# Working out a token's norm, exponentials and gate where its expert works on it, and not where its attention row is finished

## The chip, the cores and the metric

The kernel runs on one core of one Trainium2 chip, as one launch. The metric is the device time of that launch in microseconds (us), lower is better. A run's time is that of the whole program; the span is the time from the first to the last instruction in the profile of one execution.

## The reference

Attention without a softmax feeds a mixture of eight experts, of which each token uses one. B = 8 batches, S = 2496 tokens, D = 256, d_qk = 64, E = 8 experts, F = 1024.

```
attn = maximum(z @ z.T / S, 0) ** 2          # per batch, 2496 x 2496, symmetric
x    = u * (attn @ v)                        # 19968 tokens x 256
xn   = x / (norm(x) + 1e-6);  en = expert_emb / (norm(expert_emb) + 1e-6)
logits = xn @ en.T / tau
e    = argmax(logits)
gate = exp(logits[e] - max) / (sum(exp(logits - max)) + 1e-9)
out  = gate * (maximum(x @ w1[e], 0) @ w2[e])
```

## The kernel before

There are two parts, one after the other. In both, values are split into a high and a low float16 half, so that a product takes three matmuls.

The attention part walks over 800 steps (b, g, s): 8 batches, 5 groups of query tokens (four of 512, one of 448), 20 blocks of 128 keys. In a step TensorE does the six matmuls of `values` into the two accumulators `acc` of the group, and, where the block isn't the transpose of one done before (`own`), the two of `scores` for a block five ahead. ScalarE takes the ReLU and the square (L303, L307), VectorE makes the halves (L314, L315). The order of the instructions on ScalarE, VectorE and SyncE is the order of the program (`manual_schedule`); nothing overtakes on these three.

When a group's last step is done, `route` gives a list of pieces, each with a number of steps after which it is put into the program: x = u * acc (`gate_x`), sum of squares for a common power of two (`squares`, `total`, `scale`), the halves (`high`, `low`), four DMA transposes into whole rows (`turn`), the logits (`logits`, `take`), the argmax (`top`), the place in the expert's list (`rank`, `place`), and then the row's norm (`sums`, `norm`, `root`, `roots`), its exponentials (`shifted`, `exps`) and its gate (`gates`). At last `scatters` writes each token's row, 256 words of x in halves and 4 of tail, to its place in the DRAM tensor `xs` by an indirect DMA of GpSimd. The pieces of one group lie over the steps of the next two and more. One PSUM bank, `psM`, serves `rank`, the scales of z and v of the next batch, and the scales of the expert weights; `pm_free` keeps these apart.

The expert part takes slots of one expert's tokens: 61 of 256 tokens (A) and then 37 of 128 (B; four more are skipped here). `slot_x` loads a slot's tokens from `xs`, transposed, and their tails (`me`); `slot_w` loads 1 MB of weights, or leaves them if the expert is the same; `slot_up` does x @ w1 into `ph` tiles of 512 columns, ScalarE the ReLU (`hh`, L919) and VectorE the low half (`hl`, L920); `slot_down` does h @ w2, VectorE multiplies by the gate from `me` (`ot`, L945), and an indirect DMA writes the rows of `out`. `slot_down(k - 1)` follows `slot_up(k)`. After each `ph` tile and each half of `slot_down`, `pop` puts the next pieces of the last groups' `route` into the program. The buffers of the expert part lie where those of attention lay.

Of the kernel before, what the change touches and what calls it, by code (L numbers as in the profile page):

```python
# [19 lines left out]
P = 128  # L20
TA, TB = 256, 128
ROW = 260
# [23 lines left out]
def relu2_attention_then_moe(ctx, tc, zT, uT, v, emb, tau, w1, w2, ident, tri, iota_e, out):  # L46
# [309 lines left out]
    def route(b, g, acc, ut):  # L356
# [5 lines left out]
        xhl = rt.tile([P, 4, 512], F16, name="xhl", tag="xhl", bufs=1)  # L362
# [3 lines left out]
        n2 = rt.tile([P, 4], F32, name="n2", tag="n2")  # L366
        row = rt.tile([P, 4, ROW + 4], F32, name="row", tag="row", bufs=3)
        rowi = row.bitcast(I32)
# [34 lines left out]
        def logits():  # L403
            pm = acc[1]
            for j in range(nj):
                for q in range(4):
                    nc.tensor.matmul(pm[:, j * 2 * E:(j + 1) * 2 * E], xhl[:, q, j * P:(j + 1) * P], enhl[:, q % 2, :],
                                     start=(q == 0), stop=(q == 3))

        def rest_scale():  # L410
# [3 lines left out]
            odn = rt.tile([P, 1], F32, name="odn", tag="odn")  # L414
            nc.vector.tensor_tensor(odn, dn, oinv, op=ALU.mult)
            epu = rt.tile([P, 1], F32, name="epu", tag="epu")
            nc.vector.tensor_tensor(epu, up, eps, op=ALU.mult)
            loc.update(odn=odn, epu=epu)

        def take():  # L420
            pv = acc[1][:, 0:nj * 2 * E].rearrange("p (j c) -> p j c", c=2 * E)
# [4 lines left out]
            sh = rt.tile([P, 4, E], F32, name="sh", tag="sh")  # L426
            nc.vector.tensor_tensor(sh[:, :nj, :], lg[:, :nj, :], m[:, :nj].unsqueeze(2).broadcast_to([P, nj, E]), op=ALU.subtract)
            loc["sh"] = sh

        def top():  # L430
            sh = loc["sh"]
            cand = rt.tile([P, 4, E], F32, name="cand", tag="cand")
            nc.vector.scalar_tensor_tensor(cand[:, :nj, :], sh[:, :nj, :], 0.0, iotd[:, :nj, :], op0=ALU.is_ge, op1=ALU.mult)
# [11 lines left out]
        def sums():  # L445
            x = rt.tile([P, 4, D], F32, name="x", tag="xt", bufs=1)
            nc.vector.tensor_tensor(x[:, :nj, :], row16[:, :nj, 0:D], row16[:, :nj, D:2 * D], op=ALU.add)
            loc["x"] = x

        def norm(j):  # L450
            def f():
                sq = rt.tile([P, D], BF16, name="sq", tag="sq", bufs=1)
                nc.scalar.activation(sq, loc["x"][:, j, :], AF.Square, accum_out=n2[:, j:j + 1])
            return f

        def root():
            loc["root"] = sqrt_of(n2[:, :nj], (P, nj), "x")

        def roots():
            loc["s"] = loc["root"]()  # L460

        def shifted():
            inv = rt.tile([P, 4], F32, name="inv", tag="inv")
            nc.vector.tensor_scalar(inv[:, :nj], loc["s"], loc["epu"], None, op0=ALU.add)
            nc.vector.reciprocal(inv[:, :nj], inv[:, :nj])
            sh = loc["sh"]
            nc.vector.tensor_tensor(sh[:, :nj, :], sh[:, :nj, :], inv[:, :nj].unsqueeze(2).broadcast_to([P, nj, E]), op=ALU.mult)

        def exps():
            ex = rt.tile([P, 4, E], F32, name="ex", tag="ex")  # L470
            nc.scalar.activation(ex[:, :nj, :], loc["sh"][:, :nj, :], AF.Exp, scale=itau)
            loc["ex"] = ex

        def gates():
            sm = rt.tile([P, 4], F32, name="sm", tag="sm")
            nc.vector.tensor_reduce(sm[:, :nj], loc["ex"][:, :nj, :], axis=AX.X, op=ALU.add)
            nc.vector.tensor_scalar_add(sm[:, :nj], sm[:, :nj], 1e-9)
            nc.vector.reciprocal(sm[:, :nj], sm[:, :nj])
            nc.vector.tensor_scalar(row[:, :nj, D:D + 1], sm[:, :nj].unsqueeze(2), loc["odn"], None, op0=ALU.mult)
            nc.vector.tensor_scalar_add(rowi[:, :nj, D + 1:D + 2], idb[:, :nj].unsqueeze(2), float(b * S + t0))  # L480
            nc.gpsimd.memset(row[:, :, D + 2:ROW], 0.0)

# [9 lines left out]
        def place():  # L492
            ob, pm = loc["ob"], loc.pop("pm")
            state["pm"] = False
            old = state["carry"]
            pos = rt.tile([P, 4, E], F32, name="pos", tag="pos")
            nc.vector.tensor_tensor(pos[:, :nj, :], pm[:, 0:nj * E].rearrange("p (j e) -> p j e", e=E),
                                    old.unsqueeze(1).broadcast_to([P, nj, E]), op=ALU.add)
            new = sml.tile([P, E], F32, name="carry", bufs=3)
            nc.vector.tensor_tensor(new, pm[:, 4 * E:5 * E], old, op=ALU.add)  # L500
            state["carry"] = new
            nc.vector.tensor_tensor(pos[:, :nj, :], pos[:, :nj, :], ob[:, 4:4 + nj, :], op=ALU.mult)  # L502
            dst = rt.tile([P, 4], F32, name="dst", tag="dst")
            nc.vector.tensor_reduce(dst[:, :nj], pos[:, :nj, :], axis=AX.X, op=ALU.add)
            dsti = rt.tile([P, 4], U32, name="dsti", tag="dsti", bufs=3)
# [281 lines left out]
    tables = {}  # L787
    tiles = cst.tile([1, 1], I32, name="tiles")
# [57 lines left out]
    nc.vector.memset(pad.bitcast(I32)[:, D + 1:D + 2], N)  # L846
# [18 lines left out]
    def pop():  # L865
        state["step"] += 1
        run(state["step"])

# [3 lines left out]
    def slot_x(k):  # L872
# [3 lines left out]
        if k < XFIRST:  # L876
            xt = mx.tile([P, 4, T], F16, name="xt16", tag="xt16")
            me = mx.tile([P, T // P, ROW - D], F32, name="me", tag="me")
        else:
            xt = mst["mr"].tile([P, 4, T], F16, name="xr16", tag="xr16")  # L880
            me = mst["mr"].tile([P, T // P, ROW - D], F32, name="mer", tag="mer")
        nc.sync.dma_start_transpose(xt, xs[bass.ds(off, T), :].bitcast(F16)[:, 0:2 * D])
        nc.sync.dma_start(me, xs[bass.ds(off, T), D:ROW].rearrange("(j p) w -> p j w", p=P))
        mst["x", k] = xt, me
# [15 lines left out]
    def slot_up(k):  # L900
        mp, T = mst["mp"], slot_of(k)[2]
        wb = mst["w"][0][k % NWB]
        xt = mst["x", k][0]
# [21 lines left out]
    def slot_down(k):  # L925
# [3 lines left out]
        me = mst.pop(("x", k))[1]  # L929
# [3 lines left out]
        for j in range(nj):  # L933
# [8 lines left out]
            pop()  # L942
        for j in range(nj):
            o = po[:, j * D:(j + 1) * D]
            nc.vector.tensor_scalar(ot[:, j, :], o, me[:, j, 0:1], ws_, op0=ALU.mult, op1=ALU.mult)  # L945
            nc.gpsimd.indirect_dma_start(  # L946
                out, bass.IndirectOffsetOnAxis(ap=me.bitcast(U32)[:, j, 1:2], axis=0),
# [142 lines left out]
    def work(k0, k1, load=True):  # L1090
# [15 lines left out]
    ks = KT - NSKIP if KB > 2 * NSKIP else KT  # L1106
# [77 lines left out]
```

## Time and profile before

| | |
|---|---|
| runs | 2192.25, 2198.60, 2198.92 us; median 2198.6 us |
| profiled execution, its own time | 2194.44 us |
| its span | 2192.3 us |
| TensorE busy | 2100.9 us (96%) |
| VectorE busy | 1420.4 us (65%) |
| ScalarE busy | 1196.4 us (55%) |
| GpSimd busy | 352.5 us (16%) |
| mean granted TensorE clock | 0.991 of 2.4 GHz |

The profile is one execution. Busy shares over the whole span mix the two parts, so they have to be taken from stretches of time: attention runs from the start to 1334.8 us, the experts from there to the end. A busy TensorE may still be slowed by its clock, which is given beside it.

### The profile page before, as it was taken

What the parts mean: (1) busy time and instruction counts of PE and PEld (TensorE: products, weight loads), DVE (VectorE), ACT (ScalarE), POOL (GpSimd) and SP (SyncE); (2) the same over time, 40 slices, a digit from 0 to 9 for tenths busy, and PEclk for the clock granted to TensorE, in tenths of its full rate; (3) what the DMA queues carried; (4) which work ended last, traced back from release to release, by engine and by line L of the source; (5) the groups of instructions that cost most, each with busy time, mean ns of one, the idle gap of its engine ahead of it and who ended that gap; (6) DMA issues with size and microseconds to landing.
All of it is one profiled execution on the core that took longest, in us unless ns stands there. A gap on an engine that the chain in (4) does not pass through costs nothing. (4 is left out here: it accounts for less than half of the span.)

```text
span 2192.3 us, 43207 instructions
## 1 busy us (share of the span) xinstructions
PE 2100.9 (96%) x15154; PEld 1345.3 (61%) x15154; DVE 1420.4 (65%) x3796; ACT 1196.4 (55%) x2329; POOL 352.5 (16%) x428
## 2 busy tenths in 40 slices
PE   6999999999999999999999999999999999999997
PEld 2444444444444444444444446888888888889996
DVE  7788878888889878798888864543333333333332
ACT  6778768768868858768869762222222222221221
POOL 0011111111111111111111111221111111111111
PEclk9999999999999999999999999999999999999999
DMA  6766957975975965966976647443233332237360
GB/s 165 176 145 191 197 140 187 189 207 129 222 196 129 244 158 128 239 170 181 202 185 148 145 104 208 112 118 72 50 91 94 88 88 52 52 112 203 92 164 27
DMA packets 610316, 317.85 MB, mean 145 GB/s; under 512 B 530981, under 2 KB 573486, under 8 KB 602928
## 3 DMA queue, kind: packets, MB, share of 16 engines
q1 hardware_dynamic: 594912, 273.82, 53.5%
q0 software_dynamic: 15184, 41.24, 6.0%
q8 instruction: 121, 1.98, 0.4%
q14 instruction: 99, 0.81, 0.1%
HBM read 297.95 MB, written 59.60 MB: 163 GB/s over the span
## 5 line engine op out<-in xcount | busy, mean ns | idle before, releaser
L303 ACT ACTIVATE a<-sc 128x512 f32<-128x512 f32 (+1 forms) x480 | 277.7, 579 | 86.0 <-PE sc L301 81.7
L307 ACT ACTIVATE a<-a 128x512 f32<-128x512 f32 (+1 forms) x480 | 300.6, 626 | 15.1
L344 PEld LDWEIGHTS <-vv 128*128 128x128 f16 x1520 | 149.1, 98 | 193.3 <-issue 18.1
L512 POOL DMA_INDIRECT xs<-row,dsti x160 | 179.2, 1120 | 517.2 <-DMA xs<-row,dsti 314.5
L346 PEld LDWEIGHTS <-vv 128*128 128x128 f16 x1520 | 149.4, 98 | 181.9 <-issue 13.2
L940 PE MATMUL po<-w,hh 128*128 128x256 f16 x944 | 257.3, 273 | 0.0
L941 PE MATMUL po<-w,hl 128*128 128x256 f16 x944 | 257.3, 273 | 0.0
L939 PE MATMUL po<-w,hh 128*128 128x256 f16 x944 | 257.3, 273 | 0.0
L345 PEld LDWEIGHTS <-vv 128*128 128x128 f16 x1520 | 149.1, 98 | 164.2 <-issue 6.9
L946 POOL DMA_INDIRECT out_dram<-ot,mer x153 | 148.7, 972 | 606.6 <-DVE ot L945 379.9
L344 PE MATMUL acc<-tt,vv 128*128 128x512 f16 (+1 forms) x640 | 238.1, 372 | 3.5 <-DVE lg L423 2.2
L345 PE MATMUL acc<-tt,vv 128*128 128x512 f16 (+1 forms) x640 | 238.1, 372 | 0.0
L346 PE MATMUL acc<-tt,vv 128*128 128x512 f16 (+1 forms) x640 | 237.9, 372 | 0.0
L300 PE MATMUL sc<-z 128*128 128x512 f16 (+1 forms) x480 | 182.9, 381 | 14.0 <-ACT a L303 9.2
L945 DVE TENSOR_SCALAR ot<-po,mer,w 128x256 f32<-128x256 f32 x114 | 58.1, 541 | 200.0 <-PE po L941 197.4
L301 PE MATMUL sc<-z,z 128*128 128x512 f16 (+1 forms) x480 | 182.8, 381 | 0.0
L941 PEld LDWEIGHTS <-hl 128*128 128x128 f16 x1272 | 124.5, 98 | 14.4
L940 PEld LDWEIGHTS <-hh 128*128 128x128 f16 x1272 | 124.5, 98 | 14.0
L939 PEld LDWEIGHTS <-hh 128*128 128x128 f16 x1272 | 124.5, 98 | 14.0
L440 POOL MEMSET ob<- 128x72 bf16 x40 | 6.2, 158 | 642.8 <-DVE pos L502 594.9
L939 PE MATMUL po<-wb,hh 128*128 128x256 f16 x328 | 89.4, 273 | 0.0
L940 PE MATMUL po<-wb,hh 128*128 128x256 f16 x328 | 89.4, 273 | 0.0
(4162 smaller groups left out, 5144.9 us busy)
## 6 DMA issues: line engine op xcount, KB each, us to landing
w<-wsd SPq DMA_DIRECT2D x73, 1026.0 KB
wa<-wsd SPq DMA_DIRECT2D x50, 1024.0 KB
w<-wsd SPq DMA_DIRECT2D x48, 1024.0 KB
wb<-wsd SPq DMA_DIRECT2D x25, 1026.0 KB
scan<-in_v_dram SPq DMA_DIRECT2D x56, 312.0 KB
vt<-in_v_dram SPq DMA_DIRECT2D x133, 128.0 KB
ut<-in_uT_dram SPq DMA_DIRECT2D x32, 512.0 KB
wr<-in_w_dram SPq DMA_DIRECT2D x16, 1024.0 KB
```

The costliest lines, as they stand in the source:

```text
L300: nc.tensor.matmul(sc[:, :n], z1[:, ss], z1[:, t0:t0 + n], start=True, stop=False)
L301: nc.tensor.matmul(sc[:, :n], z1[:, ss], z2[:, t0:t0 + n], start=False, stop=True)
L303: nc.scalar.activation(a[:, :n], sc[:, :n], AF.Relu, scale=2.0 ** -SHIFT)
L307: nc.scalar.activation(a[:, :n], a[:, :n], AF.Square)
L344: nc.tensor.matmul(acc[k][:, :n], va, ph[:, :n], start=first, stop=False)
L345: nc.tensor.matmul(acc[k][:, :n], va, pl[:, :n], start=False, stop=False)
L346: nc.tensor.matmul(acc[k][:, :n], vb, ph[:, :n], start=False, stop=last)
L512: nc.gpsimd.indirect_dma_start(xs[:, :], bass.IndirectOffsetOnAxis(ap=loc["dsti"][:m, j:j + 1], axis=0), row[:m, j, 0:ROW], None)
L939: nc.tensor.matmul(o, hh[:, f, t], wh, start=(f == 0), stop=False)
L940: nc.tensor.matmul(o, hh[:, f, t], wl, start=False, stop=False)
L941: nc.tensor.matmul(o, hl[:, f, t], wh, start=False, stop=(f == NF - 1))
L946: nc.gpsimd.indirect_dma_start(out, bass.IndirectOffsetOnAxis(ap=me.bitcast(U32)[:, j, 1:2], axis=0), ot[:, j, :], None, bounds_check=N - ...
```

## The change

Attention ends with a row's shifted logits, its scale factors and its token number in a longer tail (`ROW` grows from 260 to 268 words: 8 shifted logits `SH`, the factor `ODN`, the epsilon `EPU`, the token `ID`). The pieces `sums`, `norm`, `root`, `roots`, `shifted`, `exps` and `gates` leave `route`; their work is done in the expert part by `gate_pieces`, for 256 tokens at a time, from whole rows that `slot_rows` loads from `xs`. These pieces are put into the program one at each `pop`, beginning with the slot before the one that they belong to. The remaining pieces of `route` get other steps, `xhl` gets a second buffer, `row` goes from three to two, and the logits go to the bank `psM` and no longer to the group's second accumulator.

```diff
-ROW = 260
+SH, ODN, EPU, ID, ROW = 256, 264, 265, 266, 268
@@ route
-        xhl = rt.tile([P, 4, 512], F16, name="xhl", tag="xhl", bufs=1)
+        xhl = rt.tile([P, 4, 512], F16, name="xhl", tag="xhl")
-        row = rt.tile([P, 4, ROW + 4], F32, name="row", tag="row", bufs=3)
+        row = rt.tile([P, 4, ROW + 4], F32, name="row", tag="row")
+        tail = rt.tile([P, 4, ROW - D], F32, name="rtail", tag="rtail")
@@ logits
-            pm = acc[1]
+            pm = psM.tile([P, 512], F32, name="pm", tag="m")
...
+            state["pm"] = True
@@ rest_scale
-            nc.vector.tensor_tensor(odn, dn, oinv, op=ALU.mult)
-            nc.vector.tensor_tensor(epu, up, eps, op=ALU.mult)
+            for c, x, y in ((ODN, dn, oinv), (EPU, up, eps)):
+                nc.vector.tensor_tensor(tail[:, :, c - D], x.broadcast_to([P, 4]), y.broadcast_to([P, 4]), op=ALU.mult)
+            nc.vector.tensor_scalar_add(tail.bitcast(I32)[:, :, ID - D], idb, float(b * S + t0))
@@ sums, norm, root, roots, shifted, exps, gates removed
+        def ends():
+            nc.gpsimd.memset(tail[:, :, ID - D + 1:], 0.0)
+            nc.gpsimd.tensor_copy(row[:, :nj, D:ROW], tail[:, :nj, :])
-        return [(0, gate_x), (4, squares), (7, total), (9, scale), (11, high), (13, low), (15, turn), (17, logits),
-                (18, rest_scale), (19, take), (20, top), (23, rank, True), (25, place), (34, sums)] \
-            + [(36 + j, norm(j)) for j in range(nj)] \
-            + [(41, root), (42, roots), (43, shifted), (46, exps), (48, gates), (49, scatters)]
+        return [(0, gate_x), (4, squares), (9, total), (11, scale), (13, high), (15, low), (17, turn), (19, logits, True),
+                (20, rest_scale), (22, take), (23, top), (26, rank, True), (29, place), (33, ends), (34, scatters)]
@@ pop
         run(state["step"])
+        if gateq:
+            gateq.pop(0)()
@@ slot_x: no more me; for k >= XFIRST it calls slot_rows(k, off)
+    def slot_rows(k, off=None):
...
+        if j0 == 0:
+            mst["me", g] = mst["mr"].tile([P, 2, ROW], F32, name="me", tag="me")
+        nc.sync.dma_start(mst["me", g][:, j0:j0 + T // P, :], xs[bass.ds(off, T), :].rearrange("(j p) w -> p j w", p=P))
+    def gate_pieces(g):
...
+        def sums():
+            nc.vector.tensor_tensor(x[:, :n, :], me16[:, :n, 0:D], me16[:, :n, D:2 * D], op=ALU.add)
+        def norms():
+            for j in range(n):
+                nc.scalar.activation(sq, loc["x"][:, j, :], AF.Square, accum_out=loc["n2"][:, j:j + 1])
+        def root():
+            loc["root"] = sqrt_of(loc["n2"][:, :n], (P, n), "x%d" % n)
+        def roots():
...
+            nc.scalar.activation(ex[:, :n, :], ex[:, :n, :], AF.Exp, scale=itau)
+        def gates():
...
+        return [sums, norms, root, roots, gates]
@@ slot_down
+        while ("gate", g) not in mst:
+            gateq.pop(0)()
-            nc.vector.tensor_scalar(ot[:, j, :], o, me[:, j, 0:1], ws_, op0=ALU.mult, op1=ALU.mult)
+            nc.vector.tensor_scalar(ot[:, j, :], o, sm[:, j0 + j:j0 + j + 1], ws_, op0=ALU.mult, op1=ALU.mult)
@@ pm_free
-        return not state["pm"] and not any(takes and due <= i + 1 for due, _, takes in queue)
+        return not state["pm"] and not any(takes and due <= i + 3 for due, _, takes in queue)
@@ after the last step of attention
     for k in range(2, NWB):
         slot_w(k, 0)
         slot_w(k, 1)
+        slot_rows(k - 2)
         slot_x(k + 1)
+    slot_rows(2)
@@ work
+            if k == k0:
+                gates_of(k, k1)
+            gates_of(k + 1, k1)
             slot_up(k)
```

## Rows read from the trace of the kernel before

**Rows 1.** Windows: length, busy us of PE, PEld, DVE, ACT, POOL, clock, DMA, GB/s.

```profile
100.00:1300.00 1200.00, 1148.75 (x6053) 534.94 (x6052) 1007.18 (x2964) 908.26 (x1812) 179.83 (x237) 0.99 0.74 175
1100.00:1300.00 200.00, 199.27 (x1062) 93.70 (x1061) 162.71 (x502) 150.13 (x298) 32.44 (x43) 1.00 0.63 148
1400.00:2100.00 700.00, 700.00 (x6954) 633.82 (x6952) 259.70 (x453) 160.83 (x275) 139.02 (x144) 1.00 0.38 94
```

**Rows 2.** Waits of PE, 100 to 1330 us: total, times, longest.

```profile
PE acc L382 <- ACT xhl L378: 10.7, 9, 2.2
PE sc L300 <- ACT a L303: 9.2, 12, 1.8
PE acc L407 <- DVE xhl L396: 5.3, 4, 1.7
PE pm L562 <- DVE pos L502: 3.8, 2, 3.5
PE pm L487 <- DVE wm L550: 3.3, 1, 3.3
...
PE pm L544 <- DVE pos L502: 0.4, 1, 0.4
```

**Rows 3.** Windows of 20 us in attention with a granted clock below 1.

```profile
260.00:280.00 20.00, 16.47 (x90) 7.63 (x89) 18.40 (x67) 8.37 (x21) 3.19 (x5) 0.92 0.78 166
...
660.00:680.00 20.00, 17.78 (x89) 8.52 (x88) 18.42 (x63) 15.07 (x35) 0.16 (x1) 0.91 0.63 169
```

**Rows 4.** Lines of ACT, 100 to 1330 us: count, busy us, mean ns, idle before.

```profile
L453 ACT ACTIVATE sq<-x 128x256 bf16<-128x256 f32 x152 | 61.1, 402 | 11.2 <-DVE x L447 10.9
...
L378 ACT ACTIVATE xhl<-xt 128x1024 f16<-128x1024 f32 x31 | 32.7, 1056 | 51.7 <-DMA row<-xhl 30.6 <-DVE xt L374 13.5 <-DVE xt L689 5.1
...
L453 ACT ACTIVATION_READ_ACCUMULATOR sq<-x 128x1 f32 x152 | 28.3, 186 | 0.0
...
L471 ACT ACTIVATE ex<-sh,itau 128x32 f32<-128x32 f32 x37 | 11.6, 315 | 28.1 <-DVE sh L467 27.9
```

**Rows 5.** Lines of DVE, 100 to 1330 us.

```profile
L447 DVE TENSOR_TENSOR x<-row 128x1024 f32<-128x1024 f16 x38 | 46.3, 1218 | 0.0
...
L691 DVE SCALAR_TENSOR_TENSOR xt<-xt,xn2c 128x4 f32<-128x4 f32 x111 | 18.0, 162 | 3.8
...
L464 DVE TENSOR_SCALAR inv<-xs,epu 128x4 f32<-128x4 f32 x37 | 8.4, 227 | 0.8
```

**Rows 6.** Timeline of PE where attention ends: start, us, instruction, [idle before].

```profile
1334.45 0.35 PE L342 MATMUL acc<-hl__16666,vv 128*128 128x448 f16 x1
1337.57 0.27 PE L915 MATMUL ph__17106<-xt,wa 128*128 128x256 f16 x1 [2.77 <-DMA xt<-xs]
...
1350.43 0.27 PE L915 MATMUL ph__17295<-xt,wa 128*128 128x256 f16 x1 [1.05 <-DVE hl L920]
```

**Rows 7.** Windows of 1 us after attention ends.

```profile
1339.00:1340.00 1.00, 1.00 (x7) 0.72 (x5) 0.00 (x0) 0.32 (x1) 0.00 (x0) 0.50 0.65 116
...
1353.00:1354.00 1.00, 1.00 (x11) 0.90 (x10) 0.90 (x6) 0.00 (x0) 0.00 (x0) 1.00 1.10 451
```

**Rows 8.** Timeline of SyncE's queue there, and the landing of the tails.

```profile
1347.03 2.04 SPq L896 DMA_DIRECT2D w<-wsd  x3
...
1352.55 2.45 SPq L883 DMA_DIRECT2D mer<-xs  x1
...
DMA to landing us min/median/max: 2.9/3.7/4.0
```

**Rows 9.** Lines of DVE, 1400 to 2100 us, shapes apart.

```profile
L945 DVE TENSOR_SCALAR ot<-po,mer,w 128x256 f32<-128x256 f32 x100 | 50.5, 541 | 180.9 <-PE po L941 178.2 <-DMA mer<-xs 2.6
...
L920 DVE SCALAR_TENSOR_TENSOR hl<-ph__18488,hh 128x512 f16<-128x512 f32 x1 | 0.7, 693 | 0.9 <-ACT hh L919 0.9
```

**Rows 10.** Windows among A slots and among B slots.

```profile
1500.00:1600.00 100.00, 100.00 (x919) 89.63 (x917) 35.38 (x57) 21.49 (x36) 17.91 (x19) 1.00 0.25 58
...
2050.00:2090.00 40.00, 40.00 (x537) 37.83 (x535) 14.45 (x24) 8.96 (x15) 6.80 (x7) 1.00 0.46 106
```

More of the change, by code (lines that the diff above doesn't have):

```diff
@@ L365, in route @@
         lg = rt.tile([P, 4, E], F32, name="lg", tag="lg")
-        n2 = rt.tile([P, 4], F32, name="n2", tag="n2")
-        row = rt.tile([P, 4, ROW + 4], F32, name="row", tag="row", bufs=3)
-        rowi = row.bitcast(I32)
+        row = rt.tile([P, 4, ROW + 4], F32, name="row", tag="row")
+        tail = rt.tile([P, 4, ROW - D], F32, name="rtail", tag="rtail")
+        sh = tail[:, :nj, SH - D:ODN - D]
         row16 = row.bitcast(F16)
@@ L443, in top @@
             loc["ob"] = ob
[L445 to L481, printed above, removed]
         def rank():
@@ L504, in place @@
             nc.vector.tensor_reduce(dst[:, :nj], pos[:, :nj, :], axis=AX.X, op=ALU.add)
-            dsti = rt.tile([P, 4], U32, name="dsti", tag="dsti", bufs=3)
+            dsti = rt.tile([P, 4], U32, name="dsti", tag="dsti")
             nc.vector.tensor_copy(dsti[:, :nj], dst[:, :nj])
             loc["dsti"] = dsti
+        def ends():
+            nc.gpsimd.memset(tail[:, :, ID - D + 1:], 0.0)
+            nc.gpsimd.tensor_copy(row[:, :nj, D:ROW], tail[:, :nj, :])
         def scatters():
@@ L883, in slot_x @@
-        nc.sync.dma_start(me, xs[bass.ds(off, T), D:ROW].rearrange("(j p) w -> p j w", p=P))
-        mst["x", k] = xt, me
+        pool = mx if k < XFIRST else mst["mr"]
+        xt = pool.tile([P, 4, T], F16, name="xt16" if k < XFIRST else "xr16", tag="xt16")
+        nc.sync.dma_start_transpose(xt, xs[bass.ds(off, T), :].bitcast(F16)[:, 0:2 * D])
+        mst["x", k] = xt
+        if k >= XFIRST:
+            slot_rows(k, off)
+    def slot_rows(k, off=None):
+        tab, i, T = slot_of(k)
+        if off is None:
+            off = nc.sync.value_load(tab[0:1, 0, i:i + 1], min_val=0, max_val=E * CAP + TB - T)
+        g, j0, n = pair_of(k)
+        if j0 == 0:
+            mst["me", g] = mst["mr"].tile([P, 2, ROW], F32, name="me", tag="me")
+        nc.sync.dma_start(mst["me", g][:, j0:j0 + T // P, :], xs[bass.ds(off, T), :].rearrange("(j p) w -> p j w", p=P))
@@ new lines, in pair_of @@
+    def pair_of(k):
+        if k < KA:
+            return k, 0, 2
+        k0 = KA if k < KLAST else KLAST
+        k1 = KLAST if k < KLAST else KT
+        g = k0 + (k - k0) // 2 * 2
+        return g, k - g, min(2, k1 - g)
+    def gate_pieces(g):
+        n = pair_of(g)[2]
+        mp, me = mst["mp"], mst["me", g]
+        loc = {}
+        def sums():
+            me16 = me.bitcast(F16)
+            x = mp.tile([P, 2, D], F32, name="gx", tag="gx")
+            nc.vector.tensor_tensor(x[:, :n, :], me16[:, :n, 0:D], me16[:, :n, D:2 * D], op=ALU.add)
+            loc["x"] = x
+        def norms():
+            loc["n2"] = mp.tile([P, 2], F32, name="gn", tag="gn")
+            for j in range(n):
+                sq = mp.tile([P, D], BF16, name="gsq", tag="gsq")
+                nc.scalar.activation(sq, loc["x"][:, j, :], AF.Square, accum_out=loc["n2"][:, j:j + 1])
+        def root():
+            loc["root"] = sqrt_of(loc["n2"][:, :n], (P, n), "x%d" % n)
+        def roots():
+            s = loc["root"]()
+            inv = mp.tile([P, 2], F32, name="ginv", tag="ginv")
+            nc.vector.tensor_tensor(inv[:, :n], s, me[:, :n, EPU], op=ALU.add)
+            nc.vector.reciprocal(inv[:, :n], inv[:, :n])
+            ex = mp.tile([P, 2, E], F32, name="gex", tag="gex")
+            nc.vector.tensor_tensor(ex[:, :n, :], me[:, :n, SH:SH + E], inv[:, :n].unsqueeze(2).broadcast_to([P, n, E]),
+                                    op=ALU.mult)
+            nc.scalar.activation(ex[:, :n, :], ex[:, :n, :], AF.Exp, scale=itau)
+            loc["ex"] = ex
+        def gates():
+            sm = mp.tile([P, 2], F32, name="gsm", tag="gsm", bufs=3)
+            nc.vector.tensor_reduce(sm[:, :n], loc["ex"][:, :n, :], axis=AX.X, op=ALU.add)
+            nc.vector.tensor_scalar_add(sm[:, :n], sm[:, :n], 1e-9)
+            nc.vector.reciprocal(sm[:, :n], sm[:, :n])
+            nc.vector.tensor_tensor(sm[:, :n], sm[:, :n], me[:, :n, ODN], op=ALU.mult)
+            mst["gate", g] = sm
+        return [sums, norms, root, roots, gates]
@@ L886, in slot_w, with gates_of @@
+    gateq = []
+    def gates_of(k, k1):
+        if k < k1 and pair_of(k)[1] == 0:
+            gateq.extend(gate_pieces(k))
     def slot_w(k, i):
@@ L942, in slot_down @@
             pop()
+        while ("gate", g) not in mst:
+            gateq.pop(0)()
+        sm, me = mst["gate", g], mst["me", g]
         for j in range(nj):
             o = po[:, j * D:(j + 1) * D]
-            nc.vector.tensor_scalar(ot[:, j, :], o, me[:, j, 0:1], ws_, op0=ALU.mult, op1=ALU.mult)
+            nc.vector.tensor_scalar(ot[:, j, :], o, sm[:, j0 + j:j0 + j + 1], ws_, op0=ALU.mult, op1=ALU.mult)
             nc.gpsimd.indirect_dma_start(
-                out, bass.IndirectOffsetOnAxis(ap=me.bitcast(U32)[:, j, 1:2], axis=0),
+                out, bass.IndirectOffsetOnAxis(ap=me.bitcast(U32)[:, j0 + j, ID:ID + 1], axis=0),
                 ot[:, j, :], None, bounds_check=N - 1, oob_is_err=False)
@@ L1085, in relu2_attention_then_moe, with work @@
         slot_w(k, 1)
+        slot_rows(k - 2)
         slot_x(k + 1)
+    slot_rows(2)
     for k in range(NWB + 1, XAHEAD):
         slot_x(k)
-    def work(k0, k1, load=True):
+    def work(k0, k1):
         for k in range(k0, k1):
```

30 lines of the change are left out of this document (11 added, 19 removed).

## The prediction

> **What bounds the kernel now.** I read the windows first, because the two parts have different limits. In the expert part TensorE is busy for the whole of 700 us, VectorE for 37% and ScalarE for 23% of it [rows 1]: that part lasts as long as its matmuls, and work put on the other two engines costs nothing as long as it fits beside them. In attention, TensorE is idle for 1200 - 1148.75 = 51.3 us, while VectorE is busy for 84% and ScalarE for 76%. In the last batch, where no next batch is scanned and split and no expert weights are prepared, it is idle for 0.7 us in 200. So attention is bound by TensorE too, with small holes while it shares the other engines with preparation.
>
> The second view is who TensorE waited for [rows 2]. Four kinds are to be seen. `total` waits for `squares` on ScalarE (10.7 us). The scores wait for a free PSUM buffer, that is for ScalarE's ReLU (9.2). The logits wait for `low` (5.3). The users of the one bank `psM` wait until VectorE has read it for the user before: eight rows from 3.8 down to 0.4 us, 14.2 in all. The rest, some 12 us, is spread over waits of VectorE's halves and of `ob`.
>
> The third view is the granted clock. Five 20 us windows of attention show less than 1, from 0.92 in the first to 0.91 in the last [rows 3]; one of them shows 0.83. What is missing in them adds up to 0.52 x 20 = 10.4 us of work at the full level. The holes and these spells, 62 us, are all that attention can give.
>
> The fourth is the seam of the two parts: the last attention matmul begins at 1334.45, the first expert one at 1337.57 after 2.77 us idle for the first tokens [rows 6]. The clock then stands at 0.50, the lower of its two levels, for about 3.3 us [rows 7], which costs half of that, 1.7. Two more holes, the second of 1.05 at 1350.43 [rows 6], take 1.6. Together the seam costs 6.0 us.
>
> **What attention loses.** Per group of 512 tokens, ScalarE drops four squares with their readouts and one exponential: 4 x (0.402 + 0.186) + 0.315 = 2.67 us, and with it the time for which it stood waiting for VectorE in front of them, (10.9 + 27.9) / 38 = 1.0 us [rows 4]. VectorE drops the addition of the halves, 1.22 us, and 20 small instructions (13 of the root, 3 of `shifted`, 4 of `gates`; the token number only moves) at 0.162 to 0.227 [rows 5]: 20 x 0.175 = 3.5, together 4.7 us. Over 38 groups in this stretch that is 139 us of ScalarE, waits included, and 179 us of VectorE; their shares fall to some 64% and 69%. GpSimd's clearing of 8 words gives place to a clearing and a copy of 48; no row has that copy, and I bound it by nothing and by VectorE's addition of 1024, 1.2 us. GpSimd is busy for 15%, its queue has 15 steps less to wait for, and nothing waits for a scatter before the experts, so it costs nothing at either end.
>
> Three edits of the schedule matter as much. `xhl` with two buffers removes the wait of `squares` for the transposes of the group before, 30.6 us in which ScalarE stands still with ReLUs queued behind it [rows 4]. `total` comes five steps after `squares` instead of three; a step is some 1.6 us ((1335 - 20) / 800), so even the longest wait, 2.2, fits in. And `pm_free` keeps the bank free for three steps ahead of `logits` and `rank`, where it was one.
>
> Term by term, of the waits in [rows 2]: of 10.7 I take 9 as gone; of 9.2, which come from a full ScalarE, 6; of 5.3, 3, as the distance from `low` to `logits` stays; of 14.2 at the bank, 8 (the 3.3 before `rank` goes by `pm_free`, the others shrink as VectorE lags less); of the other 12, 5. That is 31. Against it stands that 38 times the logits use the bank, which they did not; at the price of today's uses (14.2 us over about 100 of them, 0.14 each) up to 5 us, and nothing if the three free steps do their work: I take 3. Of the clock's 10.4 I take 5, since the longest hole, 3.5 at the bank before `L562`, need not go. Attention: -31 + 3 - 5 = -33 us. Ends: all of the 62 gone, or only the 9 and the 3.3, with 5 back, -7.
>
> The pieces that need the bank may now begin in only 6 of 20 steps (a take lies from step 16 of a group to step 28). The preparation of weights then halts for up to 14 steps and catches up at one piece a step. The bunched pieces are ReLU-sized work on both engines; I count that inside the terms that I left standing.
>
> **What the experts gain in work.** For 256 tokens VectorE gets an addition of 512 columns, half of 1.22 by estimate, and the 20 small instructions, 3.7 with their spacing: 4.3 us. It has four `hl` and two `ot`, 4 x 0.69 + 2 x 0.54 = 3.85 [rows 9]. Together 8.2 us. An A slot has 96 matmuls, and 919 take 100 us: 10.45 us. Two B slots have 144, and 537 take 40: 10.7 [rows 10]. So VectorE would be busy for 78%, and ScalarE, with 1.5 us more, for 38%. The round trips (`norms` wait for `sums`, `root` for `norms`, the exponential for `roots`, `gates` for the exponential) hold the next `hl` back by 2 to 3 us, and a slot's `hl` is wanted only when the next slot's `slot_up`, 5.2 us of matmuls, is done. Cost nothing; cover gone when VectorE's work and waits pass the slot. The row reads add 1072 bytes a token, 21 MB in 850 us, beside 94 GB/s that flow at a DMA share of 0.38 [rows 1]: no cost.
>
> **What the seam gets.** The scatter that `slot_x(0)` waits for lies 15 steps earlier, so the 2.77 and the clock behind it go, and with the second `xhl` so does about 0.5. A new wait comes instead. After the last step, at T, SyncE issues three loads of 1 MB and only then the rows of slot 0; `sums` of slot 0 stands in VectorE's queue right behind the first `hl`, at T + 2.8, and `norms` in ScalarE's. The three loads take 2.04 us to issue [rows 8], flow at some 400 to 450 GB/s [rows 7], 7.5 us, and begin 2 us after issue, so the rows land at about T + 11. Behind `sums` are queued the second `hl` and all that follow. Three `ph` buffers rotate (at 1350.43 the eighth tile waited for the fifth one's `hl` [rows 6]), so TensorE does four tiles, 5.2 us, and then stands. Then VectorE works off its queue: `hl`, `take` and `top` of a late group, `root`, `roots`, `gates`, some 2 us between one `hl` and the next. By that count the second `slot_up` ends at T + 22.5 and not at T + 10.5: 12 us, and 1 more behind it. The seam goes from 6.0 to 13: +7.
>
> The Trainium skill, "DMA: Bandwidth & Descriptors", section "Queues, rings and completion order", says that each DMA engine takes the descriptors of a ring in order, which puts the rows behind the 3 MB. The landing of the tails, 2.9 to 4.0 us with three weight loads just ahead, doesn't show such a delay, but the tail issued at 1352.55 was itself held for 2.45 us [rows 8]. By the rule the seam is +7; by the landing times alone the rows would be there at T + 6 and the seam +1.
>
> I take +7 without that rule as well: the flow in those windows is at its highest while the loads last. Ends: 0 and +15 (rows that also wait for the last scatters, T + 16 or later).
>
> **The sum.** -33 + 7 = -26 against the profiled execution's 2194.4 (span 2192.3 and 2.1 around it), 2168.4. That execution lies 4.2 below the median of the runs, so 2172 on their scale.
>
> **The rivals.**
> *All holes close and the seam is hidden.* Attention -52 (ten of the 62 left), seam 0: 2146. For it: the last batch runs at 99.6% with VectorE at 81% and ScalarE at 75% [rows 1]. Against it: that batch has no scans, no next batch's splits and no weights, and their late DMAs hold ScalarE and VectorE up whatever the load. 0.12.
> *The bank takes the place of the load.* 38 more uses, halted preparation in bunches and a seam of +12 leave -14 + 12, about 2196, no change. For it: the last batch has VectorE just as full and no holes, so load alone isn't the cause, and the bank's waits are the largest kind. 0.21.
> *The expert part becomes bound by VectorE.* Place: `gates` and `root` in VectorE's queue, waiting for ScalarE. It decides once waits pass 10.45 - 8.2 = 2.25 us in a slot. At 2.75 a slot it costs 0.5 x 61 for the A slots and 0.5 x 18 for pairs of B slots, +39: 2211, slower. Against it: `hl` has a slot of slack. 0.12.
> The forecast, 2160 to 2184, has 0.55.
>
> **How the numbers follow.** About 0.3%, 6.6 us, is what a measurement of this kernel can tell from no change. Faster: 0.55 + 0.12 + half of the second rival, 0.78; same: 0.10, nearly all of the second rival's other half; slower: 0.12. The range 2148 to 2198 takes in the forecast with its bounds and the second rival, and leaves out the third and half of the first, 0.18.
>
> **What would show it.** Right: in 100 to 1300 us TensorE idle some 20 to 25 us instead of 51; no wait of L378 for row transposes; VectorE near 70% there and near 75% among the experts, with TensorE still at 100%; a hole of several us in the first two `slot_up`, ended by `hl`, with `sums` waiting for `me`. Wrong: holes at `pm` as long as before (second rival), holes at `ph` in every slot (third), or no hole at the seam (first).

## The result and the profile after

The changed kernel takes 2173.81 us (median of 4 runs, 2171.31 to 2179.27) against 2197.85 us for the kernel before on the same chip: a ratio of 0.9899, with a 95% interval of 0.9874 to 0.9924. It is faster by 24.0 us. The forecast was 2172, that is -26. The profiled execution is the one of 2171.31 us, with a span of 2169.5.

Cut at the start of the last attention matmul, which I call T, the two halves of the sum stand apart. T was 1334.45 us [rows 6] and is 1302.48: -32.0. The rest, the span less T, was 857.9 and is 867.0: +9.1.

Windows of the kernel after, with the columns of [rows 1]: all of attention that answers to the first row there, the same up to T, the experts, and a stretch of A slots as in [rows 10].

```profile
100.00:1300.00 1200.00, 1170.58 (x6232) 551.04 (x6230) 873.66 (x2243) 856.81 (x1506) 188.76 (x284) 0.99 0.80 180
100.00:1302.48 1202.48, 1173.06 (x6259) 552.51 (x6257) 873.66 (x2243) 856.81 (x1506) 189.67 (x285) 0.99 0.80 180
1400.00:2100.00 700.00, 700.00 (x7064) 635.10 (x7062) 491.61 (x1804) 230.67 (x598) 134.45 (x136) 1.00 0.47 119
1500.00:1600.00 100.00, 100.00 (x919) 89.62 (x917) 69.86 (x255) 33.15 (x85) 18.70 (x19) 1.00 0.39 97
```

TensorE's idle time in 100 to 1300 fell from 51.3 us [rows 1] to 29.4. VectorE's share fell from 84% to 73%, ScalarE's from 76% to 71%. Among the experts VectorE went from 37% to 70%, and TensorE is still busy for all 700 us. An A slot lasts as long as before: 919 matmuls in 100 us, as in [rows 10].

The kernel before, the window from 100 us to its own T, for comparison with the second row:

```profile
100.00:1334.45 1234.45, 1183.20 (x6261) 552.54 (x6260) 1024.46 (x3027) 923.52 (x1847) 184.64 (x244) 0.99 0.73 174
```

For the same 6260 matmuls, to within two, idle time fell by 1234.45 - 1183.20 - 29.42 = 21.8 us, and busy time by 1183.2 - 1173.1 = 10.1. Together that is the 32.0.

Most of the 10.1 are pauses too. Matmuls of 512 columns are drawn 0.38 us long, but start 0.22 us apart; two of the kernel before:

```profile
620.26 0.38 PE L345 MATMUL acc<-hl__7623,vv 128*128 128x512 f16 x1
620.48 0.38 PE L346 MATMUL acc<-hl__7623,vv 128*128 128x512 f16 x1
```

So of each pause the first 0.16 us does not show as idle. Counted from the starts in both traces (behind matmuls of 512 and 448 columns, at the full clock, more than 0.02 us late), there are 97 late starts before and 39 after, and the part of them that does not show as idle is 13.0 us and 4.9. That is 8.1 of the 10.1.

Waits of TensorE in the kernel after, 100 to 1350 us; the columns are those of [rows 2].

```profile
PE pm L448 <- DVE ob L440: 13.8, 7, 2.9
PE ph__15486 L946 <- DVE hl L951: 9.9, 1, 9.9
PE sc L300 <- ACT a L303: 4.5, 6, 2.0
PE pm L407 <- ACT xhl L393: 4.4, 1, 4.4
PE pm L407 <- DVE xhl L396: 2.3, 2, 1.9
PE ph__15775 L946 <- DVE hl L951: 1.6, 1, 1.6
PE acc L382 <- ACT xhl L378: 0.9, 1, 0.9
PE pm L507 <- DVE pos L463: 0.7, 1, 0.7
```

`total`'s wait and nearly all waits of one user of the bank for the one before are gone. One wait has grown: `rank` (L448) waits for VectorE's `ob`, 13.8 us, where the kernel before has 2.6:

```profile
PE pm L487 <- DVE ob L441: 2.6, 4, 1.2
```

The second and sixth rows belong to the seam of the two parts. How they come about is in four timelines of the kernel after, with the columns of [rows 6]. TensorE's has the hole:

```profile
1318.84 0.37 PE L946 MATMUL ph__15486<-xt,wa 128*128 128x256 f16 x1 [9.89 <-DVE hl L951]
...
1321.35 0.42 PE L946 MATMUL ph__15506<-xt,wa 128*128 128x256 f16 x1
```

VectorE's shows what stood in front of that `hl`:

```profile
1304.87 0.69 DVE L951 SCALAR_TENSOR_TENSOR hl<-ph__15339,hh 128x512 f16<-128x512 f32 x1 [1.22 <-ACT hh L950]
1317.49 0.69 DVE L877 TENSOR_TENSOR gx<-me 128x512 f32<-128x512 f16 x1 [11.93 <-DMA me<-xs]
1318.10 0.68 DVE L951 SCALAR_TENSOR_TENSOR hl<-ph__15356,hh 128x512 f16<-128x512 f32 x1
...
1319.64 0.69 DVE L951 SCALAR_TENSOR_TENSOR hl<-ph__15381,hh 128x512 f16<-128x512 f32 x1
```

SyncE's has the loads of the weights and of the rows:

```profile
1302.89 2.02 SPq L927 DMA_DIRECT2D w<-wsd  x3
1314.57 0.39 SPq L857 DMA_DIRECT2D me<-xs  x1
```

Its wait in front of the second:

```profile
SPq L857 <- DMA xs<-row,dsti: 8.7, 1, 8.7
```

And GpSimd's has the scatters that the rows waited for:

```profile
1298.72 0.99 POOL L477 DMA_INDIRECT xs<-row,dsti  x1 [11.10 <-DMA xt<-xs]
...
1311.59 0.96 POOL L477 DMA_INDIRECT xs<-row,dsti  x1 [6.01 <-DMA xs<-row,dsti]
```

The `sums` of slot 0 (L877) stand in VectorE's queue behind the first `hl` and wait 11.93 us for `me`. The rows of `me` are not even asked for until 1314.57, T + 12, though the three weight loads are issued at 1302.89. SyncE stands for 8.7 us behind the scatter of the third of the last batch's five groups (its step 34 is six steps before attention ends; those of the last two groups come later): GpSimd issued its first part only at 1298.72, after an `xt` load that reads the same array, and its last part at 1311.59. The first three parts are issued 3 us apart, the last 7 us behind the third, while the weights flow; that these slow it is not tested.

### The profile page after: what moved, and what is told of

The parts are those of the page before. It is cut to its first block, busy times and chain, and to the rows that moved or that the text cites. A ratio compares the mean times of both kernels' runs of the same rounds, so it can differ in the third digit from the quotient of the medians.

```text
span 2169.5 us, 44194 instructions
## 1 busy us (share of the span) xinstructions
PE 2092.6 (96%) x15154; PEld 1346.2 (62%) x15154; DVE 1545.5 (71%) x4636; ACT 1210.1 (56%) x2367; POOL 358.4 (17%) x468
## 5 line engine op out<-in xcount | busy, mean ns | idle before, releaser
L980 POOL DMA_INDIRECT out_dram<-ot,me x159 | 157.2, 989 | 646.6 <-DVE ot L979 331.8
L477 POOL DMA_INDIRECT xs<-row,dsti x160 | 171.3, 1070 | 430.8 <-DMA xs<-row,dsti 352.5
L897 ACT ACTIVATE gex<-gex,itau 128x16 f32<-128x16 f32 x80 | 24.6, 307 | 260.0 <-DVE gex L895 251.6
L972 PEld LDWEIGHTS <-hl 128*128 128x128 f16 x1272 | 124.5, 98 | 14.4
L884 ACT ACTIVATE gsq<-gx 128x256 bf16<-128x256 f32 x159 | 64.8, 408 | 48.4 <-DVE gx L877 44.0
L971 PE MATMUL po<-wb,hh 128*128 128x256 f16 x328 | 89.4, 273 | 0.0
L972 PE MATMUL po<-wb,hl 128*128 128x256 f16 x328 | 89.4, 273 | 0.0
```

Of the source, the lines that this page charges most:

```text
L477: nc.gpsimd.indirect_dma_start(xs[:, :], bass.IndirectOffsetOnAxis(ap=loc["dsti"][:m, j:j + 1], axis=0), row[:m, j, 0:ROW], None)
L971: nc.tensor.matmul(o, hh[:, f, t], wl, start=False, stop=False)
L972: nc.tensor.matmul(o, hl[:, f, t], wh, start=False, stop=(f == NF - 1))
L980: nc.gpsimd.indirect_dma_start(out, bass.IndirectOffsetOnAxis(ap=me.bitcast(U32)[:, j0 + j, ID:ID + 1], axis=0), ot[:, j, :], None, bounds ...
```

## The experiments

All ratios are against the kernel before, run on the same chip as the experiment; its medians were 2195.53, 2195.93 and 2197.11 us in the three batches of runs. Differences of medians between rows of the table go across chips, on which the kernel before differs by 2.3 us (2195.53 to 2197.85).

| kernel | median us | ratio (95% interval) | T | span less T |
|---|---|---|---|---|
| before (profiled run) | 2197.85 | 1 | 1334.45 | 857.9 |
| after | 2173.81 | 0.9899 (0.9874 to 0.9924) | 1302.48 | 867.0 |
| e2_schedule_alone | 2244.97 | 1.0221 (1.0197 to 1.0246) | 1387.19 | 862.2 |
| e1_second_xhl | 2242.12 | 1.0211 (1.0191 to 1.0230) | 1381.90 | 858.6 |
| e16_two_rows | 2244.55 | 1.0222 (1.0205 to 1.0239) | 1381.39 | 859.7 |
| e11_move_alone | 2166.24 | 0.9873 (0.9854 to 0.9891) | 1295.95 | 868.5 |
| e5_one_xhl | 2184.29 | 0.9935 (0.9918 to 0.9952) | 1313.29 | 869.8 |
| e4_rank_later | 2163.56 | 0.9859 (0.9841 to 0.9878) | 1296.53 | 868.2 |
| e3_rows_with_x | 2169.38 | 0.9891 (0.9873 to 0.9908) | 1304.31 | 862.9 |
| e12_scatter_later | 2165.87 | 0.9868 (0.9851 to 0.9885) | 1301.12 | 862.0 |
| e8_rows_and_rank | 2159.40 | 0.9848 (0.9829 to 0.9867) | 1292.76 | 862.6 |
| e13_three_edits | 2150.49 | 0.9792 (0.9777 to 0.9807) | 1295.39 | 854.0 |
| e15_old_order_seam | 2154.24 | 0.9804 (0.9788 to 0.9820) | 1296.13 | 856.3 |
| e6_root_twice | 2276.14 | 1.0356 (1.0334 to 1.0378) | 1302.47 | 973.9 |

T and the span less T are of the one profiled execution. The kernels after, e3, e6 and e12 have the same order of work in attention but for e12's scatters, and their T spread over 3 us, from 1301.12 to 1304.31, so differences of T below that say nothing.

### Where attention's gain comes from: the moved work or the schedule

**e2_schedule_alone**: the kernel before with the changed schedule; the gate stays in attention.

```diff
-        xhl = rt.tile([P, 4, 512], F16, name="xhl", tag="xhl", bufs=1)
+        xhl = rt.tile([P, 4, 512], F16, name="xhl", tag="xhl")
-        row = rt.tile([P, 4, ROW + 4], F32, name="row", tag="row", bufs=3)
+        row = rt.tile([P, 4, ROW + 4], F32, name="row", tag="row")
...
-            pm = acc[1]
+            pm = psM.tile([P, 512], F32, name="pm", tag="m")
...
-                (18, rest_scale), (19, take), (20, top), (23, rank, True), (25, place), (34, sums)] \
+                (20, rest_scale), (22, take), (23, top), (26, rank, True), (29, place), (36, sums)] \
...
-        return not state["pm"] and not any(takes and due <= i + 1 for due, _, takes in queue)
+        return not state["pm"] and not any(takes and due <= i + 3 for due, _, takes in queue)
```

> The kernel before with the new order of the pieces, the second xhl, the logits in the one bank and three free steps there, but norm, exponentials and gate stay in attention. Theory (both the lighter engines and the order matter): attention gives about half of the 33 us, no new hole at the seam, ratio to before 0.991 to 0.996. Rival (the order alone does it): attention gives the whole 33 us and the seam loses nothing, ratio 0.983 to 0.986. Second rival (the lighter engines alone do it): ratio 0.998 or more.

It was slower, by 49 us, which only the second rival's "or more" covers, and not for its reason. The room for the second `xhl` had come from the third `row`, so this run has two suspects more than it was made for.

**e1_second_xhl**: the kernel before with those two buffer counts alone.

```diff
-        xhl = rt.tile([P, 4, 512], F16, name="xhl", tag="xhl", bufs=1)
+        xhl = rt.tile([P, 4, 512], F16, name="xhl", tag="xhl")
-        row = rt.tile([P, 4, ROW + 4], F32, name="row", tag="row", bufs=3)
+        row = rt.tile([P, 4, ROW + 4], F32, name="row", tag="row")
```

> The kernel before with a second buffer for xhl (and row with two in place of three, to make the room). Theory: squares stop waiting for the row transposes (30.6 us of ScalarE), total's 10.7 us of waits fall to 3 or less, 8 to 14 us less than before, ratio 0.9935 to 0.9965. Rival (ScalarE then waits for the next late thing, and TensorE with it): ratio 0.998 to 1.002.

It lost 46 us, which neither expectation has.

**e16_two_rows**: only the second of the two lines.

> The kernel before with two row buffers in place of three, nothing else. If the loss of the two kernels that kept the gate in attention (46 and 49 us) comes from SyncE waiting at the row transposes for the scatter of two groups before, this kernel loses as much: ratio to before 1.015 to 1.025. If it comes from their other edits (second xhl, new order), this one stays at 0.998 to 1.004.

`row` alone makes all of the loss: 2244.55 us against 2242.12 with both lines, the intervals overlap. SyncE's longest wait in e16_two_rows, 100 to 1330 us:

```profile
SPq L401 <- DMA xs<-row,dsti: 149.2, 47, 10.1
```

TensorE's longest there:

```profile
PE acc L382 <- ACT xhl L378: 32.2, 9, 8.8
```

The transposes into `row` (L401) wait for the scatters out of the buffer of two groups before, 149 us in all, and every other transfer of SyncE waits behind them; the kernel before has no such row. The second `xhl` next to it moved T by 0.5 us, nothing. The new order on top of both (e2 against e1) moved T by +5.3. So e1 and e2 do not show the schedule at work in a healthy kernel, and the split had to be made from the other side.

**e11_move_alone**: the kernel after, with the moved work but the order, the one `xhl`, the logits' place and the free step of before. `ends` and `scatters` stay at 33 and 34, and `row` at two buffers.

```diff
-        xhl = rt.tile([P, 4, 512], F16, name="xhl", tag="xhl")
+        xhl = rt.tile([P, 4, 512], F16, name="xhl", tag="xhl", bufs=1)
...
-            pm = psM.tile([P, 512], F32, name="pm", tag="m")
+            pm = acc[1]
...
-        return [(0, gate_x), (4, squares), (9, total), (11, scale), (13, high), (15, low), (17, turn), (19, logits, True),
-                (20, rest_scale), (22, take), (23, top), (26, rank, True), (29, place), (33, ends), (34, scatters)]
+        return [(0, gate_x), (4, squares), (7, total), (9, scale), (11, high), (13, low), (15, turn), (17, logits),
+                (18, rest_scale), (19, take), (20, top), (23, rank, True), (25, place), (33, ends), (34, scatters)]
...
-        return not state["pm"] and not any(takes and due <= i + 3 for due, _, takes in queue)
+        return not state["pm"] and not any(takes and due <= i + 1 for due, _, takes in queue)
```

> The changed kernel with the old order of the pieces that stay in attention: one xhl, logits in the accumulator, total three steps after squares, one free step at the bank. Norm, exponentials and gate are in the expert part. Theory (the lighter ScalarE and VectorE close most holes by themselves): attention 18 to 28 us shorter than before, seam as in the changed kernel, ratio to before 0.990 to 0.996. Rival (it takes the new order as well): attention less than 10 us shorter, ratio 0.999 to 1.004. Second rival (the new order costs time even with the lighter engines): as fast as the changed kernel or faster, 0.985 to 0.990.

The ratio is the second rival's. T fell to 1295.95, 38.5 us below before and 6.5 below after. The moved work alone gives all of attention's gain; the new order takes some 6 us of it back. That rests on T: the intervals of the two ratios overlap, but the four kernels with the new order have T from 1301.12 to 1304.31, and the two with the old one (e15, below, is the other) 1295.95 and 1296.13. TensorE's waits in e11_move_alone, 100 to 1350 us:

```profile
PE acc L382 <- ACT xhl L378: 10.1, 8, 2.6
...
PE acc L407 <- DVE xhl L396: 3.0, 2, 2.2
PE pm L521 <- DVE pos L459: 2.6, 1, 2.6
...
PE sc L300 <- ACT a L303: 2.3, 1, 2.3
```

The bank's waits and those of the scores went without the new order. `total`'s 10.1 stayed, and the 13.8 of `rank` are not there.

**e5_one_xhl**: the kernel after with one `xhl` (the first line of the diff above).

> The changed kernel with one xhl buffer. If the second buffer was worth the 9 us that the prediction gave it, this is 6 to 12 us slower than the changed kernel: ratio to before 0.9925 to 0.9955. If the five steps between squares and total cover the wait, or the lighter ScalarE does, no change: 0.988 to 0.991.

T rose by 10.8 us, to 1313.29, and the ratio is the one expected if the second buffer is worth its 9 us. Waits of ScalarE in e5_one_xhl, 100 to 1330 us:

```profile
ACT xhl L378 <- DMA row<-xhl: 118.6, 20, 13.2
```

With `turn` two steps later, the squares of the next group meet the transposes of the one before. The second `xhl` is needed by the new order. With the old order it is worth nothing: e15_old_order_seam (below) has it, with edits at the seam beside it, and its T is 1296.13 against 1295.95.

**e4_rank_later**: the kernel after with `rank` and `place` three steps later.

```diff
-                (20, rest_scale), (22, take), (23, top), (26, rank, True), (29, place), (33, ends), (34, scatters)]
+                (20, rest_scale), (22, take), (23, top), (29, rank, True), (32, place), (33, ends), (34, scatters)]
```

> The changed kernel, with rank at step 29 and place at step 32, where they were at 26 and 29. Theory (TensorE waits there only because top is late): the 13.8 us of waits for ob fall below 3, 10 to 15 us less than the changed kernel, ratio 0.983 to 0.986. Rival (VectorE is late by a fixed amount of work and the wait turns up at the next piece or at other users of the bank): waits of the same sum under other names, ratio 0.989 to 0.991.

T fell by 6.0 us to 1296.53, and the median by 10.3; the ratio's interval ends at 0.9878, just inside that of after. The ratio is the theory's, but both expectations are half right: the wait for `ob` is gone from TensorE's list, and in its place come 7.3 us at `total` and 7.4 at L507. In the timeline of the kernel after, the seven waits of `rank` lie about one batch apart; two of them:

```profile
333.17 0.27 PE L448 MATMUL pm<-ob,ones_b 128*128 128x40 bf16 x4 [2.19 <-DVE ob L440]
501.24 0.27 PE L448 MATMUL pm<-ob,ones_b 128*128 128x40 bf16 x4 [2.86 <-DVE ob L440]
```

VectorE's timeline in front of the second of them:

```profile
495.17 1.28 DVE L374 TENSOR_TENSOR xt<-acc,ut 128x512 f32<-128x512 f32 x2
496.37 0.61 DVE L315 TENSOR_TENSOR hl__5585<-a,hl__5585 128x448 f16<-128x448 f32 x1
496.90 0.87 DVE L284 SCALAR_TENSOR_TENSOR vv<-vt,scv,vv 128x256 f16<-128x256 f32 x2
...
498.71 0.19 DVE L424 COPY lg<-pm 128x32 f32<-128x32 f32 x1
...
499.49 0.68 DVE L498 TENSOR_REDUCE mx<-wr 128x1 f32<-128x512 f32 x1
...
500.99 0.19 DVE L440 TENSOR_TENSOR ob<-iot,m 128x32 bf16<-128x32 f32 x1
```

In front of each of the seven VectorE prepares the next batch's `vv` and `z` without a gap, in front of four a part of an expert weight as well, and `take` and `top` stand among these.

### What the seam waits for

**e3_rows_with_x**: the rows of slots 0 and 1 are loaded together with their tokens, ahead of the weights, into scan buffers that are free by then (these get a pool of their own).

```diff
...
+            if k < 2:
+                t = scp.tile([P, SCAN], F32, name="me0", tag="scan")
+                mst["me", g] = t[:, 0:2 * ROW].rearrange("p (j w) -> p j w", w=ROW)
...
             slot_x(k)
+        for k in range(2):
+            slot_rows(k)
...
-        slot_rows(k - 2)
```

> The changed kernel, with the whole rows of slots 0 and 1 loaded together with their transposed tokens, 11 steps before attention ends. Theory (VectorE stands still for rows that land late): the hole of 9.9 us and the low clock after it go, TensorE idle under 3 us between the parts, 12 to 17 us less than the changed kernel, ratio to before 0.982 to 0.985. Rival (the backlog of gate pieces and late pieces of attention fills VectorE there anyway): 0 to 4 us less, ratio 0.988 to 0.990.

The hole of 9.9 us shrank to 1.2, as the theory has it, but the rest (the span less T) fell by 4.1 us, not by the whole hole, and the ratio is the rival's: 3.3 us came back at `ph__15942`, because the next load of SyncE (L845, tokens of a later slot, with the rows of slot 2 behind it) now stood 12.0 us for the same scatter. SyncE's wait in e3_rows_with_x:

```profile
SPq L845 <- DMA xs<-row,dsti: 12.0, 1, 12.0
```

**e12_scatter_later**: the kernel after with the scatters at 42.

```diff
-                (20, rest_scale), (22, take), (23, top), (26, rank, True), (29, place), (33, ends), (34, scatters)]
+                (20, rest_scale), (22, take), (23, top), (26, rank, True), (29, place), (33, ends), (42, scatters)]
```

> The changed kernel with scatters at step 42 where it was 34, so that the loads of the first rows come before the last batch's third scatter in the program. If the rows of slot 0 are late because SyncE waits for that scatter, they land 4 to 5 us earlier (then behind the three weight loads), the hole of 9.9 us shrinks to 4 to 6, the low clock after it shortens, 4 to 9 us less than the changed kernel, ratio 0.985 to 0.988. If the 3 MB of weights ahead are what holds them, nothing changes: 0.989 to 0.991.

The scatter of the last batch's third group now comes behind those reads. The rest fell by 5.0 us; the median is 7.9 lower, with intervals that overlap. The timeline of SyncE in e12_scatter_later:

```profile
1301.50 2.02 SPq L927 DMA_DIRECT2D w<-wsd  x3
1304.33 0.39 SPq L857 DMA_DIRECT2D me<-xs  x1
```

And that of VectorE:

```profile
1312.95 0.69 DVE L877 TENSOR_TENSOR gx<-me 128x512 f32<-128x512 f16 x1 [8.75 <-DMA me<-xs]
```

With T at 1301.12, the rows are asked for at T + 3.2 and used at T + 11.8. From issue to use they take 8.6 us right behind the three weight loads; in the kernel after, asked for 11.7 us after the first of these was issued, 1317.49 - 1314.57 = 2.9. The hole that is left, 6.7 us, is theirs; 4 to 6 were expected.

**e8_rows_and_rank** is e3 and e4 together, **e13_three_edits** these two and the scatters at 42, **e15_old_order_seam** is e11 with e3's edits, the second `xhl` and the scatters at 42.

> Both of these edits. If the two holes are independent, the gains add: 22 to 32 us less than the changed kernel, ratio 0.975 to 0.980. If one hides behind the other, no more than the better one alone.

> The changed kernel with rank later, the rows of slots 0 and 1 loaded with their tokens, and scatters at step 42. If the hole that the early rows left behind (3 us in slot 3, for the rows of slot 2) comes from the same scatter, the time from the last attention matmul to the end falls from 862.6 to 856 to 859 us; ratio to before 0.979 to 0.983, the fastest so far. If it comes from VectorE's queue, no change against 0.985.

> The moved work with the old order of the remaining pieces, a second xhl, the rows of slots 0 and 1 loaded with their tokens and scatters at step 42. If order and seam are independent: the attention of the old order (last matmul at 1296 or, if the second xhl helps, 1288) and 854 to 858 us behind it, ratio to before 0.976 to 0.982, as fast as the three edits or faster. If the old order's early row transposes collide with the later scatters, SyncE waits there and the ratio is above 0.985.

e8 keeps e3's rest and has a T as low as any, but the gains do not add as expected: its median is 14.4 us below that of after, not 22 to 32. The ratios of e13 and e15 came out as expected. In e13 the seam is closed: windows of e13_three_edits.

```profile
1290.00:1390.00 100.00, 98.64 (x912) 85.70 (x910) 77.15 (x317) 32.24 (x88) 21.21 (x23) 1.00 0.69 187
```

TensorE is idle for 1.4 us there at a granted clock of 1.00; in the kernel after, 1300 to 1400 has 11.8 idle and 0.93. At 2150.49 us e13 beats both kernels, by 45 us the one before on its chip and by some 23 the one after. e15, at 2154.24, is not told apart from it: with the seam closed, the old order and the new one with `rank` at 29 are worth the same.

### How much room VectorE has left among the experts

**e6_root_twice**: the kernel after with the root of each slot worked out a second time, its result unused; 13 small instructions more on VectorE.

```diff
             loc["root"] = sqrt_of(loc["n2"][:, :n], (P, n), "x%d" % n)
+            sqrt_of(loc["n2"][:, :n], (P, n), "r%d" % n)()
```

> The changed kernel with every square root of the expert part worked out twice (13 more VectorE instructions for 256 tokens, some 2.5 us with their spacing; the second result is not used). Theory (the expert part is covered as long as VectorE's work fits into a slot of 10.45 us, of which it fills 7.3): TensorE stays at 100%, 0 to 6 us slower than the changed kernel, ratio 0.989 to 0.993. Rival (waits for ScalarE already fill the rest of the slot): 1 us and more for each of 80 pieces of 256 tokens, ratio above 1.02.

It costs 102 us, as the rival has it. T is the same to 0.01 us; all of it lies in the expert part. Windows of e6_root_twice, the experts and a stretch of A slots:

```profile
1400.00:2100.00 700.00, 633.43 (x5930) 559.05 (x5928) 556.10 (x2395) 187.01 (x532) 119.89 (x122) 1.00 0.40 102
1500.00:1600.00 100.00, 90.95 (x822) 80.19 (x820) 80.45 (x351) 25.69 (x74) 16.72 (x17) 1.00 0.31 71
```

One exponential of ScalarE in its timeline:

```profile
1530.10 0.31 ACT L898 ACTIVATE gex<-gex,itau 128x16 f32<-128x16 f32 x1 [6.34 <-DVE gex L896]
```

The same step in the kernel after:

```profile
1521.58 0.31 ACT L897 ACTIVATE gex<-gex,itau 128x16 f32<-128x16 f32 x1 [3.21 <-DVE gex L895]
```

VectorE is busy for only 80%, and yet TensorE stands for 66.6 us in 700. ScalarE's exponential waits 6.34 us for VectorE's root, the `hh` behind it in ScalarE's queue wait with it, VectorE then waits for `hh` before its `hl`, and TensorE for both. VectorE's work and its waits for ScalarE form one chain per slot, in program order; the chain, not the busy share, must fit into the slot. In the slot of e6 from 1519.61 us on VectorE stands still twice, 0.91 us for `hh` and 0.37 for the exponential, and the other 10.3 of 11.6 us are its own instructions with their spacing:

```profile
1523.31 0.69 DVE L952 SCALAR_TENSOR_TENSOR hl<-ph__19181,hh 128x512 f16<-128x512 f32 x1 [0.91 <-ACT hh L951]
```

From two `ot` that follow each other in the timelines, the slot grew from 1533.49 - 1523.01 = 10.48 to 1531.23 - 1519.61 = 11.62 us. The 13 instructions take 0.195 each with their spacing (28.5 us busy and 6.2 idle before, over 177 of L656), 2.5 us, and 11.62 - 2.5 = 9.1. By this estimate the kernel after has some 1.4 us of a slot left.

## Why the prediction was right

**Attention, -33 forecast, -32.0 measured.** The mechanism held: with the moved work alone TensorE waits less (e11). Several sizes did not. Idle time was to fall by 31 - 3 = 28 us and fell by 21.8. From [rows 2] and the waits after: `total` -9.8 (forecast -9), the scores -4.7 (-6), the wait for the splits +1.4, from 5.3 to 4.4 + 2.3 (-3), the bank from 14.2 to about 1 and so -13 (-8, with +3 for the logits that use it now). The step that failed in its size is "of the other 12, 5": `ob` is among these, and `rank`'s wait for it grew to 13.8, which no term has. So TensorE's idle time in 100 to 1300, 29.4 us, lies outside the 20 to 25 that were to show the forecast right. The clock gave 1.6 instead of 5: windows of 20 us still lack 8.8 us in all. Against these two misses stand 8.1 us of pauses that the idle view could not show. That the sum came within 1 us is luck: errors of both signs cancelled.

The loads fell less than forecast. Up to T, ScalarE's busy time fell by 923.5 - 856.8 = 66.7 us and VectorE's by 1024.5 - 873.7 = 150.8, where the forecast took off 139 and 179; the shares ended at 71% and 73%, not 64% and 69%. The forecast had added drawn lengths, which overlap (L877 above is drawn 0.69 us long, and the next instruction starts 0.61 behind it), and had taken ScalarE's waits off its busy time.

**"Three edits of the schedule matter as much."** This failed. The second `xhl` and the free steps were given credit for waits that fell with the load: e11 has neither, and its T is 38.5 us below before. `pm_free` and `logits` in the bank were not tried one by one. The new order has a price of some 6 us of T (e11 and e4 against after), for which the forecast has no term.

**The experts, nothing forecast, nothing measured.** Right, and nearer the edge than 70% suggests. VectorE's work per slot is 69.86% of 10.45 = 7.3 us by busy time; with the spacing, which the forecast's 8.2 counts for the small instructions, it is 7.9, the 10.48 us of the slot less 2.6 for which VectorE stands still. The third rival named the place, `root` and `gates`, and put the point at 2.25 us more in a slot; e6 added 2.5 us at that place and had that rival's result. The estimate from e6 puts the point lower: that the kernel after stays on the good side rests on some 1.4 us.

**The seam, +7 forecast, +9.1 measured.** The mechanism was as forecast: no `hl` passes until `sums` of slot 0 have their rows. On the forecast's scale the seam after costs 6.0 + 9.1 = 15.1 us, against 13; against e13, whose seam has 1.4 us idle, it costs 867.0 - 854.0 = 13.0. The rows came at T + 15, not T + 11: of the forecast's two ways for them to be late, the one that it kept for its bound, the wait for a scatter, was what happened. Its price was less than the +15 given to it, and less than +11, which 4 us on top of the sum would make. Behind the hole TensorE waited only 1.6 us more for `hl`: one `hl` followed another after 1.5 us and more, and TensorE, at a granted clock of 0.50 from 1318 to 1324 us, took 1321.35 - 1318.84 = 2.5 us for a tile. With SyncE's wait removed (e12) the rows are used at T + 11.8, as the step had it. The Trainium skill, "DMA: Bandwidth & Descriptors", section "Queues, rings and completion order", has each DMA engine take descriptors in ring order; the 8.6 us behind the weights against 2.9 without them agree with it. They do not prove it, since loads that only share the flow would be late as well. The forecast's other count, rows at T + 6 from the tails' landing times, did not hold.

**What stays open.** Which of the new order's edits costs the 6 us is shown only for `rank`'s place. Why the old order with one `xhl`, which leaves `total` 10.1 us of waits, does as well as e4 was not taken further.

## What to carry to other kernels

When work leaves a crowded stage, the waits of its neighbours fall by themselves; test the move with the old order before the order is changed with it, for here the order alone cost some 6 us. Where a busy engine and a second one hand work to and fro in program order, count the chain of a period, waits and the spacing of small instructions included, and not the busy share: with VectorE 80% busy this kernel lost 102 us. At a seam, look for what a load must wait behind in two places, the transfers ahead of it in the queue and the writes that it depends on; closing only one moved the hole (e3) or shortened it (e12), closing both took it away (e13, e15).

## What the runs showed that was not expected

Taking one of three `row` buffers from the kernel before, an edit made only to find room, cost 47 us: a buffer that is filled by a transposing load and emptied by an indirect scatter made SyncE stand for 149 us, with every other load of the kernel behind it. The kernel after has two such buffers without that wait; its scatters come at step 34 and not at 49. Nor have e12, e13 and e15 that wait, with two buffers and the scatters at 42.
